# Batch 0's gate in one VectorE multiply in a Fourier-mixing and gated-convolution kernel

## The chip, the cores and the metric

The kernel runs on one core of one Trainium2 chip. The core has a matrix engine (TensorE, PE in the profile; its weight loads are listed apart as PEld), VectorE (DVE), ScalarE (ACT), GpSimd (POOL) and SyncE (SP), which only issues transfers. Each engine works through its own list of instructions in the order in which the program wrote them and waits on semaphores where an operand isn't ready. GpSimd also issues the transfers that accumulate into memory and those that gather by index. The metric is the device time of one execution in microseconds (us).

## The reference

Two blocks follow each other on 8 batches of 3136 x 256 float32 values. The first keeps the real part of a two-dimensional Fourier transform. The second projects to 1024 features, takes the positive part `h`, convolves it along the sequence with three taps per feature, squashes the sum with a sigmoid, multiplies that with `h` and projects back.

```python
X = np.fft.fft(np.fft.fft(x, axis=1), axis=2).real
h = np.maximum(X @ w_in, 0.0)
conv_out = sum(conv_w[k] * hp[:, k:k + S, :] for k in range(3))   # hp: h with a zero row at both ends
gate = 1.0 / (1.0 + np.exp(-conv_out))
return h * gate @ w_out
```

## The kernel before

**Transform.** The transform along the sequence is made from folded halves of `x` (VectorE adds and subtracts mirrored rows: lines 157, 160, 168, 172, 173; lines 194 and 195 make the sums and differences over features; line 228 turns two of the pieces) and from small matrix products with cosine and sine tables. Its result for one batch, the tiles `pt` and `qt`, is ready before that batch's second block starts. The transform along the features is folded into the first projection's weights, the tile `G`.

**Second block.** It is cut into steps `(b, c, f)`: batch, one of 4 chunks of the sequence, one of 8 groups of 128 features; 32 steps per batch and 256 in all. A step's tile is 128 features by 770 positions, or 832 in the last chunk of a batch. These are its parts, with their lines:

- `products` (TensorE, two matmuls into `pa` and two into `pb`), after `seed` (ScalarE, line 816) has put a first term into `pa`;
- `copies` (ScalarE, line 837, two per step) move `pb` to `nb`; `combine` (VectorE, line 845, two per step) reads `pa` from the matmul's memory and `nb`, and writes `h`, the positive part of their sums in the order of the sequence;
- the three taps: `first_tap` (ScalarE, line 851) writes `g`, `middle` (line 855) is a transfer that GpSimd issues and that adds a shifted `h` to `g` in memory, `last_tap` (VectorE, line 860) adds the last;
- `sigmoid` (ScalarE, line 875, two operations per step) and `gate`: GpSimd (line 883) multiplies one half of `g` by `h` and VectorE (line 884) the other;
- `mm2` (TensorE, 12 matmuls `po<-wout,g`) projects back; after the eighth group of features ScalarE copies `po` out (line 908).

**Order.** The order of the work is written out by hand. One loop runs over cycles `t`, and in a cycle each part belongs to another step, so that every engine finds work whose inputs came a cycle earlier:

```python
sigmoid(steps[t - 4]); products(steps[t + 1]); copies(steps[t + 1])
combine(steps[t]); seed(steps[t + 2]); first_tap(steps[t])
run("dve"); last_tap(steps[t - 3]); gate(steps[t - 4])
row_of(steps[t + 1]); middle(steps[t]); run("pool"); run("load"); mm2(steps[t - 5]); run("pe")
```

So VectorE's list in a cycle is `combine`, then side work, then `last_tap`, then `gate`. GpSimd's is `gate`, in some cycles a small `memset` (line 822), the issue of `middle`, then its own side work, among it the gathers of `x` for a later batch (line 132). Side work is hung on cycles by the table `side`. In batch 0's steps (cycles 0 to 35) it is: turning the output weights `wout` into float32 (VectorE lines 654, 662, 668, 669, 677), the folds and the products of batch 1's transform, and the first folds of batch 2's. The tiles `h` have 6 buffers and the tiles `g` 7.

Of the kernel before, what the change touches and what calls it, by code (L numbers as in the profile page):

```python
# [13 lines left out]
ALU = mybir.AluOpType  # L14
# [23 lines left out]
def kernel(  # L38
# [48 lines left out]
    vt = nc.vector.tensor_tensor  # L87
# [7 lines left out]
    def spare():  # L95

        return pso.tile([P, 2, D], F32, name="po", tag="po").rearrange("p a d -> p (a d)")
# [764 lines left out]
    def shares(s):  # L862


        ch = chunks[s[1]]
        w = ch.w - 2
        n = ch.rest[0] if ch.last else w
        m = n - n // 2
        return slice(0, m), slice(m, n), slice(n, w)

    def sigmoid(s):

        v, p, r = shares(s)
        for c in (slice(p.start, r.stop), v):
            act(gs[s][:, c], gs[s][:, c], AF.Sigmoid, scale=cw[:, 1, s[2]:s[2] + 1])  # L875

    def gate(s):

        b, c, f = s
        g, h = gs[s], hs.pop(s)[:, 1:]  # L880
        v, p, r = shares(s)
        p = slice(p.start, r.stop)
        gt(g[:, p], g[:, p], h[:, p], op=ALU.mult)  # L883
        vt(g[:, v], g[:, v], h[:, v], op=ALU.mult)  # L884
# [83 lines left out]
    for i, u in enumerate(us[j] for j in (4, 2, 3, 7, 8)):  # L968
        u.matmuls(0, 1)
        if i == 0:  # L970
            p = spare()
# [111 lines left out]
    for t in range(n + LAG):  # L1083
# [3 lines left out]
        if 0 <= t - 4 < n:  # L1087
            sigmoid(steps[t - 4])
# [17 lines left out]
        if 0 <= t - 4 < n:  # L1106
            gate(steps[t - 4])
# [75 lines left out]
```

## Time and profile before

| | |
|---|---|
| median of 3 runs | 1167.69 us (1164.38 to 1167.98) |
| the profiled execution | 1167.47 us, span of its instructions 1165.7 us |
| granted TensorE clock | 0.997 |
| TensorE busy | 1143.1 us, 98% of the span |
| VectorE busy | 978.5 us, 84% |
| ScalarE busy | 943.7 us, 81% |
| GpSimd busy | 604.7 us, 52% |
| batch 0's gates on GpSimd | 32, from 62.3 us to 203.5 us |
| batch 0's gates on VectorE | 32, from 63.2 us to 206.1 us |

An engine's busy time counts an instruction from its start to its end, and with it the time for which the instruction had started and could not go on. An idle time before an instruction is put down to the instruction that ended last of those it waited for. In rows that list instructions in order of time the columns are start (us from the span's start), duration (us), engine, line, operation, tiles and shape, how many were merged, and in brackets the idle time before with what ended it.

### The profile page before, as it was taken

To read this page: it belongs to the slowest core of one execution; us is meant where nothing else is said; L and a number is where in the kernel's file an instruction comes from. 1 tells how busy PE (TensorE), PEld (TensorE's weight loads), DVE (VectorE), ACT (ScalarE), POOL (GpSimd) and SP (SyncE) were. 2 spreads that over 40 slices of the span, in tenths; PEclk is the share of its full clock that TensorE was granted. 3 is DMA by queue.
4 is the path that set the end of the run, shared out by engine and by line. 5 is a ranking of instruction groups with operands and counts; after the bars stand their busy time and mean duration, and the time that the engine had idled before them with its cause. 6 is when DMAs were issued, how large, how long until landed. Compare 5 with 4: busy or idle time off the path is not lost.

```text
span 1165.7 us, 15936 instructions
## 1 busy us (share of the span) xinstructions
PE 1143.1 (98%) x4834; PEld 892.4 (77%) x4834; DVE 978.5 (84%) x1449; ACT 943.7 (81%) x1950; POOL 604.7 (52%) x741
## 2 busy tenths in 40 slices
PE   6989999999999999999999999999999999999998
PEld 4767787778777777778777777777777787777777
DVE  8799989997887889898877879779787777888885
ACT  3589877888888879887878888888887888898885
POOL 7356545665466464646365464745344444454443
PEclk9899999999999999999999999999999999999999
DMA  9767886777667686757675766865565556666654
GB/s 247 152 111 172 163 149 145 165 164 162 135 142 164 128 192 127 177 112 168 144 173 126 153 132 133 178 130 122 130 130 99 120 122 143 136 127 130 127 115 102
DMA packets 107602, 167.54 MB, mean 144 GB/s; under 512 B 32104, under 2 KB 62838, under 8 KB 107517
## 3 DMA queue, kind: packets, MB, share of 16 engines
q0 software_dynamic: 42160, 115.87, 52.0%
q1 hardware_dynamic: 64616, 50.53, 15.7%
q8 instruction: 38, 0.62, 0.2%
q14 instruction: 47, 0.39, 0.1%
q10 hardware_dynamic: 741, 0.14, 0.1%
HBM read 37.80 MB, written 25.74 MB: 55 GB/s over the span
## 4 chain that ended last, share of the span: by engine, by line
PE 79%; ACT 5%; DVE 4%; issue 2%; DVEq 0%; ACTq 0%
PE po L93 50%; PE pb L93 12%; PE pa L93 12%; PE pd L93 6%; DVE g L860 1%; ACT g L875 1%; ACT nb L837 1%; ACT os L908 1%; ACT pa L816 0%; DVE h L845 0%; ACT g L851 0%; DVE g L884 0%; DVE xh L168 0%; DVE w L194 0%; DVE xh L157 0%
## 5 line engine op out<-in xcount | busy, mean ns | idle before, releaser
L93 PE MATMUL po<-wout,g 128*128 128x256 f32 x3072 | 706.5, 379 | 5.3 <-DVE g L884 4.5
L93 PEld LDWEIGHTS po<-wout,g 128*128 128x128 f32 x3072 | 580.5, 190 | 150.8 <-issue 19.4
L855 POOL DMA_DIRECT2D g<-h x256 | 227.4, 888 | 470.0 <-ACT g L851 293.5
L875 ACT ACTIVATE g<-g,cw 128x385 f32<-128x385 f32 (+2 forms) x512 | 292.3, 625 | 67.2 <-DVE g L860 66.3
L883 POOL TENSOR_TENSOR g<-g,h 128x385 f32<-128x385 f32 (+1 forms) x256 | 294.5, 1151 | 44.5 <-ACT g L875 42.8
L837 ACT ACTIVATE nb<-pb 128x386 f32<-128x386 f32 (+3 forms) x512 | 227.0, 498 | 109.5 <-PE pb L93 108.9
L845 DVE CUSTOM_DVE_ANT_0 h<-pa,nb 128x386 f32<-128x386 f32 (+3 forms) x512 | 264.4, 556 | 28.1 <-POOL h L822 19.0
L860 DVE SCALAR_TENSOR_TENSOR g<-h,cw,g 128x770 f32<-128x770 f32 (+1 forms) x256 | 282.4, 1103 | 0.0
L851 ACT ACTIVATE g<-h,cw 128x770 f32<-128x770 f32 (+1 forms) x256 | 244.4, 955 | 0.0
L93 PE MATMUL pb<-qt,G 127*128 127x387 f32 (+2 forms) x512 | 214.5, 500 | 2.8 <-ACT nb L837 2.4
L93 PE MATMUL pa<-pt,G 128*128 128x387 f32 (+2 forms) x512 | 212.3, 495 | 0.5 <-ACT pa L816 0.5
L884 DVE TENSOR_TENSOR g<-g,h 128x385 f32<-128x385 f32 (+1 forms) x256 | 189.9, 742 | 24.6 <-ACT g L875 24.4
L816 ACT ACTIVATE pa<-eb,ge 128x387 f32<-128x387 f32 (+2 forms) x256 | 155.4, 607 | 1.5 <-DVE h L845 1.2
L93 PEld LDWEIGHTS pa<-pt,G 128*128 128x128 f32 x512 | 97.1, 190 | 74.7 <-issue 18.4
L132 POOL DMA_INDIRECT xh<-in_x_dram,idx x64 | 91.0, 1421 | 20.1 <-issue 11.4
L93 PEld LDWEIGHTS pb<-qt,G 127*128 127x128 f32 x512 | 91.1, 190 | 10.5 <-ACT nb L837 5.0
L93 PE MATMUL pd<-tab,w 98*128 98x197 f32 (+2 forms) x448 | 97.7, 317 | 0.2 <-DVE as L428 0.2
L93 PEld LDWEIGHTS pd<-tab,w 98*128 98x128 f32 (+1 forms) x448 | 81.9, 191 | 9.5 <-ACT pa L816 0.6
L908 ACT COPY os<-po 128x256 f32<-128x256 f32 x196 | 57.3, 393 | 6.5 <-PE po L93 6.5
L157 DVE TENSOR_TENSOR xh<-xh 98x1020 f32<-98x1020 f32 (+1 forms) x32 | 48.2, 1509 | 0.8 <-DMA xh<-in_x_dram,idx 0.7
L168 DVE TENSOR_TENSOR xh<-xh 98x1024 f32<-98x1024 f32 (+1 forms) x32 | 48.5, 1517 | 0.1
L194 DVE TENSOR_TENSOR w<-xh 98x508 f32<-98x508 f32 (+1 forms) x32 | 35.1, 1097 | 0.1
(149 smaller groups left out, 438.8 us busy)
## 6 DMA issues: line engine op xcount, KB each, us to landing
g<-h POOLq DMA_DIRECT2D x192, 385.0 KB, 4.0
g<-h POOLq DMA_DIRECT2D x64, 416.0 KB, 4.1
out_dram<-os SPq DMA_DIRECT2D x96, 256.0 KB
xh<-in_x_dram SPq DMA_DIRECT2D x16, 784.0 KB
eb<-ed SPq DMA_DIRECT2D x16, 193.5 KB
raw<-in_moe_w_in_dram SPq DMA_DIRECT2D x4, 512.0 KB
raw<-in_moe_w_out_dram SPq DMA_DIRECT2D x1, 2048.0 KB
eb<-ed SPq DMA_DIRECT2D x8, 209.0 KB
```

Of the source, the lines that this page charges most:

```text
L93: nc.tensor.matmul(o, l, r, start=start, stop=stop, skip_group_check=True)
L132: nc.gpsimd.indirect_dma_start(out=xh[b, h][0:NP, 7 - m].rearrange("p q d -> p (q d)"), out_offset=None, in_=bass.AP(tensor=x.tensor, offs ...
L816: act(pa[s][:, 0:n], eb[b, c], AF.Copy, scale=ge[:, f:f + 1])
L837: act(nb[s][:, i, cols], p[:, cols], AF.Copy, scale=-1.0 if i else 1.0)
L845: nc.vector._custom_dve(TENSOR_ADD_SAT, out=to, in0=a[:, cols], in1=c[:, i, cols], s0=BIG, s1=0.0)
L851: act(gs[s], hs[s][:, 0:n], AF.Copy, scale=cw[:, 0, s[2]:s[2] + 1])
L855: nc.gpsimd.dma_start(out=gs[s], in_=hs[s][:, 1:1 + n], accum_op=ALU.add)
L860: stt(out=g, in0=h[:, k:k + n], scalar=cw[:, k, f:f + 1], in1=g, op0=ALU.mult, op1=ALU.add)
L875: act(gs[s][:, c], gs[s][:, c], AF.Sigmoid, scale=cw[:, 1, s[2]:s[2] + 1])
L883: gt(g[:, p], g[:, p], h[:, p], op=ALU.mult)
L884: vt(g[:, v], g[:, v], h[:, v], op=ALU.mult)
L908: nc.scalar.copy(out=osb[:, j % 2], in_=pt[:, j % 2])
```

## The change

For steps of batch 0 (`s[0] == 0`) the gate is one VectorE multiply over the whole tile, 770 or 832 columns, and GpSimd gets no multiply; the sigmoid of such a step is one ScalarE operation over the whole tile in place of two over its halves. Steps of batches 1 to 7 are as before.

```diff
+    def whole(s):
+
+        return s[0] == 0
+
     def sigmoid(s):
 
         v, p, r = shares(s)
-        for c in (slice(p.start, r.stop), v):
+        for c in [slice(0, r.stop)] if whole(s) else (slice(p.start, r.stop), v):
             act(gs[s][:, c], gs[s][:, c], AF.Sigmoid, scale=cw[:, 1, s[2]:s[2] + 1])
 
     def gate(s):
...
         v, p, r = shares(s)
+        if whole(s):
+            vt(g, g, h[:, 0:r.stop], op=ALU.mult)
+            return
         p = slice(p.start, r.stop)
         gt(g[:, p], g[:, p], h[:, p], op=ALU.mult)
         vt(g[:, v], g[:, v], h[:, v], op=ALU.mult)
```

Here is GpSimd's list around the gathers (L132) of the first half of batch 2's rows of `x`, some 120 to 135 us into the span; before the change it reads:

```order
L883 TENSOR_TENSOR g<-g,h 128x385
L855 DMA g<-h 128x770
L883 TENSOR_TENSOR g<-g,h 128x385
L855 DMA g<-h 128x770
L132 DMA xh<-in_x_dram,idx 98x512
L883 TENSOR_TENSOR g<-g,h 128x385
L855 DMA g<-h 128x770
```

and after it:

```order
L855 DMA g<-h 128x770 x2
L132 DMA xh<-in_x_dram,idx 98x512
L855 DMA g<-h 128x770
L132 DMA xh<-in_x_dram,idx 98x512
L855 DMA g<-h 128x770
```

The multiply is gone from every cycle; the gathers and the issues of `middle` follow each other in the same order as before.

VectorE's list at about the same place, two cycles of it (L157, L160 and L168 are folds, side work of batch 1's transform; the program's list calls the last tap a TENSOR_SCALAR and `combine` an ISA), reads before:

```order
L157 TENSOR_TENSOR xh<-xh 99x4x255
L160 TENSOR_TENSOR xh<-xh 99x8
L860 TENSOR_SCALAR g<-h,cw,g 128x770
L884 TENSOR_TENSOR g<-g,h 128x385
L845 ISA h<-pa,nb 128x386 x2
L168 TENSOR_TENSOR xh<-xh 99x1024
```

and after the change:

```order
L157 TENSOR_TENSOR xh<-xh 99x4x255
L160 TENSOR_TENSOR xh<-xh 99x8
L860 TENSOR_SCALAR g<-h,cw,g 128x770
L887 TENSOR_TENSOR g<-g,h 128x770
L845 ISA h<-pa,nb 128x386 x2
L168 TENSOR_TENSOR xh<-xh 99x1024
```

Each gate stands where it stood, with 770 columns in place of 385; nothing else moves on VectorE.

## The prediction

> **What bounds the kernel now.** I read the page's busy times first, and then busy time by stretch, cut at the starts of four `mm2` groups:
>
> ```profile
> PE 1143.1 (98%) x4834; PEld 892.4 (77%) x4834; DVE 978.5 (84%) x1449; ACT 943.7 (81%) x1950; POOL 604.7 (52%) x741
> ```
>
> ```profile
> 63.15:138.75 75.60, 71.79 (x290) 52.83 (x290) 74.77 (x108) 65.16 (x144) 44.99 (x58) 1.00 0.71 149
> 138.75:207.20 68.45, 68.45 (x304) 53.98 (x305) 61.79 (x99) 53.41 (x112) 34.41 (x45) 1.00 0.78 143
> 207.20:241.03 33.83, 32.49 (x130) 23.89 (x129) 33.03 (x44) 27.52 (x57) 21.83 (x28) 1.00 0.74 165
> ```
>
> The columns are the stretch, its length, and the busy time of PE, PEld, DVE, ACT, POOL. Over the whole run TensorE is the bound (98%). The first two stretches hold all of batch 0's gates. In the first, VectorE is busy for 74.77 of 75.60 us and TensorE stands idle for 3.8 us. In the second TensorE is never idle and VectorE has 6.7 us to spare. In the third, already batch 1, VectorE is full again and TensorE is idle for 1.3 us. Who ends TensorE's waits in the first and in the third stretch:
>
> ```profile
> PE po L93 <- DVE g L884: 2.6, 4, 1.5
> ```
>
> ```profile
> PE po L93 <- DVE g L884: 1.3, 4, 0.6
> ```
>
> It is VectorE's gate, 2.6 us in the first and 1.3 us in the third. Here are one `mm2` group each of two undisturbed cycles, then the first and the last group of the first stretch:
>
> ```profile
> 126.64 2.75 PE L93 MATMUL po<-wout,g 128*128 128x256 f32 x12
> ...
> 130.54 2.75 PE L93 MATMUL po<-wout,g 128*128 128x256 f32 x12
> ```
>
> ```profile
> 64.97 2.75 PE L93 MATMUL po<-wout,g 128*128 128x256 f32 x12
> ```
>
> ```profile
> 138.75 0.48 PE L93 MATMUL po<-wout,g 128*128 128x256 f32 x1 [0.22 <-DVE g L884]
> ```
>
> TensorE needs 3.90 us per cycle when nothing stops it; the 17 cycles from 64.97 to 138.75 took 73.8 us and not 66.3 (small products of the border features take part of the rest). So in the first stretch VectorE sets the pace, and the question is what VectorE's full 75 us consist of. The next rows are from VectorE's and GpSimd's lists in order of time:
>
> ```profile
> 130.63 2.28 DVE L168 TENSOR_TENSOR xh<-xh 99x1024 f32<-99x1024 f32 x1
> 132.84 1.01 DVE L860 SCALAR_TENSOR_TENSOR g<-h,cw,g 128x770 f32<-128x770 f32 x1
> 133.77 0.55 DVE L884 TENSOR_TENSOR g<-g,h 128x385 f32<-128x385 f32 x1
> ```
>
> ```profile
> 129.86 1.05 POOL L132 DMA_INDIRECT xh<-in_x_dram,idx  x1 [0.30 <-issue]
> 130.93 0.90 POOL L883 TENSOR_TENSOR g<-g,h 128x385 f32<-128x385 f32 x1
> ```
>
> ```profile
> 95.82 1.21 DVE L168 TENSOR_TENSOR xh<-xh 98x1024 f32<-98x1024 f32 x1
> ```
>
> The same fold of 1024 columns took 1.21 us at 95.82, with GpSimd not multiplying, and 2.28 us at 130.63. GpSimd's multiply ended at 131.83, and the fold ended 1.08 us after that: it stood still until GpSimd had finished and then ran. So "busy" VectorE time holds standstill behind GpSimd's half of the gate. Other rows show that GpSimd's issue of `middle` (L855) does not do this:
>
> ```profile
> 72.45 0.88 POOL L855 DMA_DIRECT2D g<-h  x1 [1.09 <-ACT g L851]
> ...
> 72.51 1.02 DVE L860 SCALAR_TENSOR_TENSOR g<-h,cw,g 128x770 f32<-128x770 f32 x1
> ```
>
> The last tap under it took 1.02 us, as long as without it (1.01 at 132.84).
>
> [...]
>
> **The change part by part.** *What VectorE gains.* These are the groups of the first stretch (63.1 to 139.5 us) in which an operation was held up: busy time, then the mean ns of one.
>
> ```profile
> L884 DVE TENSOR_TENSOR g<-g,h 128x385 f32<-128x385 f32 x18 | 10.6, 588 | 0.3 <-ACT g L875 0.3
> L157 DVE TENSOR_TENSOR xh<-xh 99x1020 f32<-99x1020 f32 x2 | 3.6, 1800 | 0.0
> L228 DVE SCALAR_TENSOR_TENSOR w<-w,turn,rt 98x256 f32<-98x256 f32 x2 | 3.4, 1722 | 0.0
> L168 DVE TENSOR_TENSOR xh<-xh 98x1024 f32<-98x1024 f32 x2 | 3.3, 1638 | 0.0
> L662 DVE SCALAR_TENSOR_TENSOR wout<-raw,wout 128x512 int32<-128x512 int32 x3 | 3.1, 1048 | 0.0
> L668 DVE TENSOR_SCALAR left<-raw 128x512 int32<-128x512 int32 x3 | 3.0, 996 | 0.0
> L168 DVE TENSOR_TENSOR xh<-xh 99x1024 f32<-99x1024 f32 x1 | 2.3, 2283 | 0.0
> L195 DVE TENSOR_TENSOR w<-xh 98x508 f32<-98x508 f32 x2 | 2.0, 1010 | 0.0
> L654 DVE TENSOR_SCALAR wout<-raw 128x512 int32<-128x512 int32 x3 | 1.9, 640 | 0.0
> L194 DVE TENSOR_TENSOR w<-xh 99x508 f32<-99x508 f32 x1 | 1.5, 1521 | 0.0
> ```
>
> And these are the same operations undisturbed (two groups of 73 to 80 us, and two rows in order of time):
>
> ```profile
> L662 DVE SCALAR_TENSOR_TENSOR wout<-raw,wout 128x512 int32<-128x512 int32 x1 | 0.7, 679 | 0.0
> L668 DVE TENSOR_SCALAR left<-raw 128x512 int32<-128x512 int32 x1 | 0.4, 419 | 0.0
> ```
>
> ```profile
> 119.49 0.68 DVE L195 TENSOR_TENSOR w<-xh 98x508 f32<-98x508 f32 x1
> ```
>
> ```profile
> 145.72 0.99 DVE L228 SCALAR_TENSOR_TENSOR w<-w,turn,rt 98x256 f32<-98x256 f32 x2
> ```
>
> Standstill is count times (mean less undisturbed): L884 18 x 0.04 = 0.7; L157 2 x 0.59 = 1.2 (1.21 us taken from the fold of 1024); L228 3.4 - 1.0 = 2.4; L168 2 x 0.43 + 1.07 = 1.9; L662 3 x 0.37 = 1.1; L668 3 x 0.58 = 1.7; L195 2 x 0.33 = 0.7; L654 3 x 0.22 = 0.7 (0.42 as L668); L194 0.84. The sum is 11.2 us.
>
> *What of it stays.* The gathers (L132) hold VectorE too: the fold at 130.63 began 0.28 us before the gather ended. Four of the stretch's seven gathers were running when the held operation behind them began; at 0.28 us each 1.1 us stays. The bounds are 0 and, if all seven hold for a whole gather of 1.05 us, 7.4 us.
>
> *What VectorE pays.* A multiply took 0.55 us for 385 columns (133.77) and 1.21 us for 1024 (95.82), so a column costs 0.66 / 639 us and 385 more cost 0.40 us. The upper bound is the last tap's 1.01 us for 770 columns, 0.46 more. I take 0.40, the row of the same operation. 18 gates up to 138.75 cost 7.2 us (8.3 at most). The net on VectorE is 7.2 + 1.1 - 11.2 = -2.9 us, and as VectorE sets the pace there, the `mm2` of 138.75 comes 2.9 us sooner.
>
> *The second stretch* costs nothing on the path as long as its cover holds. 14 gates there add 8 x 0.46 (832 columns) + 6 x 0.40 = 6.1 us to VectorE; the cover is its 6.7 us of idle time, and standstill that goes here too (139.5 to 206 us):
>
> ```profile
> L168 DVE TENSOR_TENSOR xh<-xh 98x1024 f32<-98x1024 f32 x2 | 3.0, 1492 | 0.0
> L194 DVE TENSOR_TENSOR w<-xh 98x508 f32<-98x508 f32 x1 | 2.2, 2220 | 0.0
> L172 DVE TENSOR_TENSOR xh<-xh 98x512 f32<-98x512 f32 x1 | 2.0, 2008 | 0.0
> ```
>
> That is 2 x 0.28 + 1.54 + 1.33 = 3.4 us (0.68 us undisturbed for the last two). Without the cover, 6.1 us would come on the path. TensorE carries the 2.9 us through this stretch.
>
> *The third stretch.* The 3.4 us lie behind 178 us, where VectorE has no idle time left, against six gates by 0.46 = 2.8 us before the last one. VectorE so enters the third stretch some 0.6 us further ahead of TensorE, and up to 1.3 us of TensorE's waits can shrink. I take 0.8 us, between 0 and 1.3.
>
> *Sigmoid in one operation.* ScalarE's list shows two halves, and one operation of the full width:
>
> ```profile
> 79.57 0.93 ACT L851 ACTIVATE g<-h,cw 128x770 f32<-128x770 f32 x1
> 81.02 1.12 ACT L875 ACTIVATE g<-g,cw 128x385 f32<-128x385 f32 x2 [0.52 <-DVE g L860]
> ```
>
> That is 0.19 us less per step for an engine which is idle before it; I take nothing for it. The gate needs the whole sigmoid, but it stands last in VectorE's cycle, behind `combine` and side work.
>
> *GpSimd* loses 32 multiplies and gets nothing; its `middle` and gathers can only be ready sooner. A gather may wait for VectorE longer (last tap and gate now follow each other for 1.8 us), and behind it waits the next `middle`, needed three cycles later, so this is hidden by more than 8 us.
>
> **Sum.** -2.9 - 0.8 = -3.7 us. The profiled execution's own time is 1167.47 us, 0.22 below the median of 1167.69; against the median this gives 1164.0 us.
>
> **The rivals.**
>
> *VectorE only gets more work (slower).* The engine that sets the pace gets 7.2 us more in the first stretch. If the standstill stays, because GpSimd's gathers and issues take the multiply's place, the `mm2` of 138.75 comes 7.2 us later, and 1.5 us may follow at 207: 1175 to 1176 us. It decides from the point where more than 4.0 of the 11.2 us stays (11.2 - 7.2). For it speaks the gather's 1.05 us ahead of the fold at 130.63; against it the undisturbed last tap beside L855, and that a gather stands in only 7 of 18 cycles.
>
> [...]
>
> *The gain is taken up elsewhere (no change).* VectorE comes free sooner but waits for `nb` and `pa` (ScalarE is busy for 65 of 75.6 us), or the lead is lost again by 207. Then it is 1166.5 to 1168.5 us. Against it: VectorE's idle time in the first stretch is 0.8 us, so ScalarE is rarely late now.
>
> *All of TensorE's idle time goes.* 3.8 + 1.3 = 5.1 us, and up to 7.5 if all that the 17 cycles took over 66.3 us goes: 1160.2 to 1162.6 us. It needs VectorE to stay ahead of TensorE in every cycle, and cycles with a fold of 1.21 us and two weight operations leave no room for it.
>
> **How the numbers follow.** About 0.3%, 3.5 us, is what a measurement of this kernel can tell from no change. My forecast has a chance of 0.55, with a range of its own of 1162.6 to 1166; two thirds of it (0.35) are beyond the 3.5 us, 0.20 within. All idle time gone has 0.08 (faster), the gain taken up 0.14 (within), more work only 0.23 (slower). So faster 0.43, same 0.34, slower 0.23. The range goes down to 1160.0, the third rival's end, and up to 1171.0: every gather holding VectorE for its whole 1.05 us adds 7.4 - 1.1 = 6.3 us to the forecast, and half of the first rival's 7.2 us on the median ends there too.
>
> **What would show it.** In the profile after: VectorE's gate at about 0.95 us for 770 columns; L168 and L157 near 1.2 us and L668 near 0.42 in all their rows; L228's pair near 1 us; TensorE's idle time before the `mm2` groups up to 139 us shrunk, and the group now at 138.75 near 135.8; the distance from there to the end as before. It would be wrong if VectorE's side work keeps its long rows with L132 or L855 in front, or if the gate over 770 columns is itself held up.

## The result

| | before | after |
|---|---|---|
| median of 12 runs | 1165.07 us | 1161.84 us |
| lowest | 1164.38 us | 1161.41 us |
| the profiled execution | 1167.47 us | 1164.74 us |

The ratio after to before is 0.9974, with a 95% interval of 0.9964 to 0.9985: 3.2 us faster, against 3.7 forecast. The time itself, 1161.84 us, is 2.2 us below the forecast's 1164.0, because the three runs that the forecast started from had a median of 1167.69 and these twelve have one of 1165.07. Nearly all runs lie on one of two levels some 3 us apart, with a mean granted clock of 0.999 to 1.0 on the lower and of 0.993 to 0.997 on the upper, so a difference in microseconds below is that between the medians of the lower levels, against the kernel before measured beside it (1161.80 and 1164.92, so -3.1 us for the change), while a ratio takes all runs.

Busy time by stretch in the profile after, cut at 63.15 us, which in both profiles lies ahead of the first `mm2` group (64.97), and at the same three groups as before (columns: stretch, length, busy PE, PEld, DVE, ACT, POOL):

```profile
63.15:136.82 73.67, 71.45 (x290) 52.93 (x291) 72.91 (x111) 62.98 (x129) 34.05 (x38) 1.00 0.71 151
136.82:205.75 68.93, 68.88 (x306) 53.70 (x305) 61.17 (x98) 50.87 (x97) 23.41 (x32) 1.00 0.79 144
205.75:238.19 32.44, 31.41 (x130) 24.14 (x128) 31.42 (x42) 27.32 (x57) 26.15 (x27) 1.00 0.78 172
```

The lengths were 75.60, 68.45 and 33.83. So the first stretch gave 1.93 us, the second cost 0.48, the third gave 1.39: 2.84 us by 238 us; the profiled executions differ by 2.73. Behind it nothing changed (924.57 us before, 924.71 after).

These are VectorE's groups of the first stretch, after (63.1 to 137.5 us; mean ns behind the busy time):

```profile
L887 DVE TENSOR_TENSOR g<-g,h 128x770 f32<-128x770 f32 x19 | 18.2, 955 | 0.6 <-ACT g L879 0.6
...
L168 DVE TENSOR_TENSOR xh<-xh 99x1024 f32<-99x1024 f32 x2 | 2.4, 1217 | 0.0
L168 DVE TENSOR_TENSOR xh<-xh 98x1024 f32<-98x1024 f32 x2 | 2.4, 1216 | 0.0
...
L157 DVE TENSOR_TENSOR xh<-xh 99x1020 f32<-99x1020 f32 x2 | 2.4, 1212 | 0.0
...
L662 DVE SCALAR_TENSOR_TENSOR wout<-raw,wout 128x512 int32<-128x512 int32 x3 | 2.0, 683 | 0.0
...
L194 DVE TENSOR_TENSOR w<-xh 98x508 f32<-98x508 f32 x2 | 1.4, 678 | 0.0
L668 DVE TENSOR_SCALAR left<-raw 128x512 int32<-128x512 int32 x3 | 1.3, 442 | 0.0
...
L228 DVE SCALAR_TENSOR_TENSOR w<-w,turn,rt 98x256 f32<-98x256 f32 x2 | 0.9, 477 | 0.0
```

Every group that was held up is at its undisturbed time: 1217 ns where it was 2283, 442 where it was 996, 477 where it was 1722. The gate takes 955 ns, 0.40 us more than its half did. Now VectorE at the end of the stretch: the gate of step 17, and the next wait; after,

```profile
133.33 0.96 DVE L887 TENSOR_TENSOR g<-g,h 128x770 f32<-128x770 f32 x1
...
142.82 0.36 DVE L401 TENSOR_TENSOR as<-as,pd 128x196 f32<-128x196 f32 x1 [3.72 <-ACT as L397]
```

and before:

```profile
138.15 0.55 DVE L884 TENSOR_TENSOR g<-g,h 128x385 f32<-128x385 f32 x1
...
145.18 0.36 DVE L401 TENSOR_TENSOR as<-as,pd 128x196 f32<-128x196 f32 x1 [0.80 <-issue]
```

The gate ends at 134.29 and not at 138.70, 4.4 us sooner, yet the `mm2` group that reads it starts only 1.93 us sooner (136.82). VectorE then waits 3.72 us where it waited 0.80. It has gained more than was forecast, and TensorE has taken less than half of it. TensorE's waits in the first stretch after (63 to 139 us) are:

```profile
PE po L93 <- DVE g L887: 1.1, 1, 1.1
PE pb L93 <- ACT nb L837: 0.7, 1, 0.7
PE pa L93 <- ACT pa L816: 0.7, 2, 0.4
```

The wait for `pb` lies ahead of the first group (63.56 us). One wait for the gate is left, before the group at 86.13, in the cycle with two weight operations and a fold. Then TensorE waits for ScalarE's `pa`, and from 108 us on it runs at its own pace, 3.90 us per cycle and what the border features add.

One wait is new in this stretch. GpSimd's small copy into the folded halves (L179, 4 columns), ScalarE behind it and TensorE behind that:

```profile
103.68 2.14 POOL L179 COPY w<-xh 98x4 f32<-98x4 f32 x1
```

```profile
105.89 0.91 ACT L222 ACTIVATE rt<-w,turn 98x256 f32<-98x256 f32 x2 [1.53 <-POOL w L181]
106.70 0.56 ACT L816 ACTIVATE pa<-eb,ge 128x387 f32<-128x387 f32 x1
```

```profile
107.32 0.92 PE L93 MATMUL pa<-pt,G 128*128 128x387 f32 x2 [0.29 <-ACT pa L816]
```

In the kernel before, the same copy took 1.38 us, ScalarE waited 0.60 us for it, and TensorE did not wait. Here it ended at 105.82, while `combine` ran (from 105.68): VectorE's fold, last tap and gate stood back to back from 102.74 on, and now it is GpSimd that is shut out.

### The profile page after: what moved, and what is told of

It is laid out like the page before. It is cut to its first block, busy times and chain, and to the rows that moved or that the text cites. A ratio compares the mean times of both kernels' runs of the same rounds, so it can differ in the third digit from the quotient of the medians.

```text
span 1163.0 us, 15837 instructions
## 1 busy us (share of the span) xinstructions
PE 1142.7 (98%) x4834; PEld 893.1 (77%) x4834; DVE 973.3 (84%) x1449; ACT 939.3 (81%) x1918; POOL 586.9 (50%) x709
## 4 chain that ended last, share of the span: by engine, by line
PE 86%; DVE 5%; ACT 4%; issue 2%; POOL 1%; DMA 1%; ACTq 0%; POOLq 0%; DVEq 0%
PE po L93 54%; PE pb L93 13%; PE pa L93 13%; PE pd L93 6%; DVE g L860 1%; ACT nb L837 1%; ACT os L915 1%; DMA xh<-in_x_dram 1%; POOL xh L132 1%; ACT g L879 1%; DVE h L845 1%; DVE g L887 1%; ACT pa L816 0%; DMA tab<-dft_seq_dram 0%; DVE g L891 0%
## 5 line engine op out<-in xcount | busy, mean ns | idle before, releaser
L879 ACT ACTIVATE g<-g,cw 128x385 f32<-128x385 f32 (+3 forms) x480 | 286.3, 647 | 54.5 <-DVE g L860 53.4
L890 POOL TENSOR_TENSOR g<-g,h 128x385 f32<-128x385 f32 (+1 forms) x224 | 261.5, 1168 | 36.4 <-ACT g L879 35.1
L891 DVE TENSOR_TENSOR g<-g,h 128x385 f32<-128x385 f32 (+1 forms) x224 | 172.3, 769 | 24.3 <-ACT g L879 24.1
L132 POOL DMA_INDIRECT xh<-in_x_dram,idx x64 | 98.3, 1536 | 19.8 <-issue 11.5
L157 DVE TENSOR_TENSOR xh<-xh 98x1020 f32<-98x1020 f32 (+1 forms) x32 | 44.0, 1377 | 0.6 <-DMA xh<-in_x_dram,idx 0.4
L168 DVE TENSOR_TENSOR xh<-xh 98x1024 f32<-98x1024 f32 (+1 forms) x32 | 43.6, 1361 | 0.1
L401 DVE TENSOR_TENSOR as<-as,pd 128x196 f32<-128x196 f32 x14 | 5.0, 358 | 38.4 <-ACT as L397 38.4
```

The lines of the kernel that those rows point to most:

```text
L132: nc.gpsimd.indirect_dma_start(out=xh[b, h][0:NP, 7 - m].rearrange("p q d -> p (q d)"), out_offset=None, in_=bass.AP(tensor=x.tensor, offs ...
```

## The experiments

The theory was: GpSimd's multiply holds up VectorE's operations (the fold of 1024 columns took 2.28 us behind it and 1.21 without it); taking the multiply away frees VectorE of standstill that is worth more than the multiply. The rivals were that ScalarE's merged sigmoid makes the gain, or GpSimd's emptier queue. Differences are to the kernel before unless said otherwise.

### Which half of the change it is

Gate alone (the sigmoid stays in halves):

```diff
-        for c in [slice(0, r.stop)] if whole(s) else (slice(p.start, r.stop), v):
+        for c in (slice(p.start, r.stop), v):
```

> Half of the change: in batch 0 VectorE multiplies the whole gate and GpSimd none, but the sigmoid stays two operations per step. Theory (VectorE's standstill behind GpSimd's multiply goes): nearly the whole gain, 2 to 3.5 us faster than before, and VectorE's folds at 1.2 us. Rival (the gain is ScalarE's, 0.19 us per step from the merged sigmoid): within 1 us of before.

Measured: -2.9 us (ratio 0.9983, 0.9971 to 0.9994; by the ratio 2.0 us). Sigmoid alone (the gate split as before):

```diff
-        if whole(s):
-            vt(g, g, h[:, 0:r.stop], op=ALU.mult)
-            return
```

> The other half: in batch 0 the sigmoid is one operation per step, and the gate is split between GpSimd and VectorE as before. Theory (standstill): within 1 us of before, with VectorE's folds held up to 2.3 us again. Rival (ScalarE's saving makes the gain): 2 to 3 us faster than before.

Measured: -0.1 us (0.9999, 0.9988 to 1.0010). The folds of 1024 columns in the two profiles (min, median and max ns), with the gate alone and then with the sigmoid alone:

```profile
L168 DVE TENSOR_TENSOR xh<-xh x6: 1214/1218/1225, 95.2 to 192.4; 98x1024 f32<-98x1024 f32 x4, 99x1024 f32<-99x1024 f32 x2
```

```profile
L168 DVE TENSOR_TENSOR xh<-xh x6: 1208/1954/2482, 93.5 to 191.1; 98x1024 f32<-98x1024 f32 x4, 99x1024 f32<-99x1024 f32 x2
```

The gain comes with the gate's half of the change, and the standstill is gone with that half alone. ScalarE's part is 0.1 to 0.2 us, too little for these runs to tell from nothing.

### Is it that GpSimd reads, or that it is busy?

A multiply on GpSimd that nobody needs is put back in the first 18 steps:

```diff
         if whole(s):
+            if steps.index(s) < 18:
+                dummy = left[:, 0:NF // 2].rearrange("p f i -> p (f i)")[:, 0:p.stop - p.start]
+                gt(dummy, h[:, p], h[:, p], op=ALU.mult)
             vt(g, g, h[:, 0:r.stop], op=ALU.mult)
             return
```

> The changed kernel, and in the first 18 steps GpSimd multiplies again where it did before, 385 columns of h by themselves into a tile that is free there; nobody needs the result. VectorE pays for the whole gate and GpSimd reads the memory as before. Theory (two readers exclude each other): the standstill of some 10 us comes back on top of VectorE's 7.2 us, so 5 to 9 us slower than before, 8 to 12 us slower than the changed kernel. Rival (the gain came from GpSimd's halves no longer being waited for, or from the merged sigmoid): within 1.5 us of the changed kernel.

Measured: +9.0 us (1.0088, 1.0068 to 1.0108; by the ratio 10.3 us), some 12 us above the changed kernel, at the upper end of what was expected or beyond it. Its six runs spread over 6 us, and the profile is of the slowest. The stretches of this profile:

```profile
65.95:147.80 81.85, 72.43 (x286) 52.69 (x287) 79.46 (x106) 61.50 (x125) 50.52 (x52) 0.98 0.62 133
147.80:220.95 73.15, 70.86 (x306) 54.84 (x305) 63.74 (x101) 51.27 (x97) 27.62 (x35) 0.98 0.73 134
```

From the first `mm2` group to that of step 17 it is 81.85 us; in the changed kernel it was 71.85 (64.97 to 136.82). Two of VectorE's operations, and the dummy multiplies themselves, in this profile (63.1 to 148 us):

```profile
L157 DVE TENSOR_TENSOR xh<-xh 98x1020 f32<-98x1020 f32 x2 | 3.8, 1892 | 0.0
...
L172 DVE TENSOR_TENSOR xh<-xh 98x512 f32<-98x512 f32 x1 | 2.1, 2097 | 0.0
```

```profile
L889 POOL TENSOR_TENSOR left<-h 128x385 f32<-128x385 f32 x17 | 25.2, 1480 | 0.1
```

VectorE stands still again (1892 ns for 1212; 2097 for 0.68 us), though at other operations, because this multiply does not wait for the sigmoid and runs at another time. GpSimd stands still too (1480 ns in the mean and 821 to 3702 ns for one and the same multiply, where that of the kernel before took 1045 in the mean), and what queues behind it is late: a copy kept ScalarE, and TensorE behind it, waiting at the start of the second stretch, which is 4.2 us longer than in the changed kernel:

```profile
153.46 0.91 ACT L222 ACTIVATE rt<-w,turn 98x256 f32<-98x256 f32 x2 [4.92 <-POOL w L181]
```

Some 3 us of the profile are TensorE's clock: it was 0.83 from 90 to 100 us and from 150 to 160 us (an estimate: 0.17 of twice 10 us), 0.98 over each of the two stretches. Another 0.7 us of the first stretch is `combine` waiting until the dummy multiply has read a buffer of `h`. So with the multiply back both engines have standstill, VectorE 1892 ns for 1212 and GpSimd 1480 for 1045; as a price of VectorE's standstill alone the 9.0 us is too high.

The same place on the queue, with a write in the multiply's stead:

```diff
-                gt(dummy, h[:, p], h[:, p], op=ALU.mult)
+                for _ in range(2):
+                    nc.gpsimd.memset(dummy, 0.0)
```

> The changed kernel, and in the first 18 steps GpSimd fills the same free tile twice with zeros (385 columns each) where it multiplied before: about as long on GpSimd's queue, but it reads nothing. Theory (only a GpSimd operation that reads the memory excludes VectorE's operations with two inputs there): within 1 us of the changed kernel. Rival (anything that GpSimd executes holds VectorE up, or GpSimd's queue sets the pace): 3 us or more slower than the changed kernel.

Measured: -2.7 us (0.9984, 0.9971 to 0.9997), 0.4 above the changed kernel. GpSimd's fills, and VectorE's folds beside them:

```profile
L890 POOL MEMSET left<- 128x385 f32 x36 | 18.6, 518 | 1.0
```

```profile
L168 DVE TENSOR_TENSOR xh<-xh x6: 1210/1214/1219, 95.7 to 192.8; 98x1024 f32<-98x1024 f32 x4, 99x1024 f32<-99x1024 f32 x2
```

GpSimd was as busy as with its multiply in the kernel before (18.6 us, where that took 18.8) and VectorE's folds show no standstill: those of 1024 columns took 1210 to 1219 ns, and L157's of 1020 columns 1208 to 1217, where two took 1892 in the mean beside the dummy multiply. For these folds, which have two inputs in memory, it is the multiply, which reads, that holds them, not a busy queue. That only operations with two inputs are held is not shown: L654 and L668, which the multiply had held up too, have one (640 and 996 ns before, 419 and 442 after the change). Beside the fills L654 still took 514 ns, one of its three rows 0.70 us, so for these the run does not show that reading is all.

### How much of VectorE's room TensorE can take

Here the other half of the product is left out in batch 0, so VectorE's gate is as short as before and GpSimd has none:

```diff
         if whole(s):
-            vt(g, g, h[:, 0:r.stop], op=ALU.mult)
+            vt(g[:, v], g[:, v], h[:, v], op=ALU.mult)
             return
```

> The changed kernel with VectorE multiplying only its old half in batch 0; the other half of the gate's product is left out, so VectorE pays nothing for what GpSimd no longer does. It asks how much of a faster VectorE TensorE can take. Theory that VectorE still sets the pace after the change: 0.40 us times 18 gates = 7.2 us more room, so 2.5 us or more faster than the changed kernel. Rival (TensorE and ScalarE now set the pace, VectorE's new room is idle time): 0.5 to 1.5 us faster than the changed kernel, from the one wait of 1.1 us on the gate that is left at 86 us.

Measured: -6.6 us (0.9941, 0.9926 to 0.9956), 3.5 us faster than the changed kernel.

```profile
64.75:133.80 69.05, 68.90 (x287) 52.63 (x286) 64.82 (x108) 61.08 (x126) 28.50 (x38) 1.00 0.74 158
133.80:202.15 68.35, 68.35 (x306) 53.87 (x304) 55.36 (x99) 50.59 (x97) 21.09 (x32) 1.00 0.78 144
202.15:234.50 32.35, 31.41 (x129) 24.14 (x128) 31.69 (x41) 27.31 (x57) 24.92 (x27) 1.00 0.79 172
```

TensorE is idle for 0.15 us of the first stretch. From `mm2` to `mm2` it takes 69.05 us, against 71.85 in the changed kernel and 73.78 before: so VectorE still set the pace in part of the stretch after the change. Two thirds of the way (2.0 of 2.8 us) are made up to the ninth group, at 98 us in the changed kernel, where its cycle is longer than 3.90 us. The first theory held, and 3.5 us is what the gate's other half still costs, its hold on GpSimd included (the small copies took 0.5 to 1.4 us in this run).

### Which steps

`whole(s)` true for the first 18 steps only, and for the last 14 of batch 0 only:

```diff
-        return s[0] == 0
+        return steps.index(s) < 18
```

> The change for batch 0's first 18 steps alone, those of the first stretch; the other 14 are split as before. Theory: the first stretch's gain as in the changed kernel, some 1.9 us at the mm2 group of step 17, and nothing or little behind it: 1.5 to 2.5 us faster than before in all. Rival (the gain is made in the third stretch, by the lead that the second gives): under 1 us faster than before.

```diff
-        return s[0] == 0
+        return 18 <= steps.index(s) < 32
```

> The change for batch 0's last 14 steps alone. Theory: no gain up to the mm2 group of step 17, then VectorE's lead into batch 1: 0.5 to 1.5 us faster than before. With the other part it should add up to the whole change, about 3.3 us. Rival (the second stretch is hidden on both sides): 0 us.

Measured: -2.2 us (0.9981, 0.9972 to 0.9991) and -0.6 us (0.9998, 0.9989 to 1.0007, by itself not clear of the noise), -2.8 together, where the whole change gave -3.1. With the first 18 the stretches took 71.89, 68.35 and 33.86 us, with the last 14 73.94, 69.04 and 32.45. So the second stretch's 0.5 us is a price of its own gates, and the third stretch's 1.4 us is their gain: the two add up within what the runs tell.

### The copies that GpSimd makes late

Batch 1's four small copies on VectorE:

```diff
-                    nc.gpsimd.tensor_copy(w[k, 0:2, qs, 0], t()[k, s:s + 2, :, 0])
+                    (nc.vector if b == 1 else nc.gpsimd).tensor_copy(w[k, 0:2, qs, 0], t()[k, s:s + 2, :, 0])
```

> The changed kernel, with the four small copies of batch 1's transform (4 columns each) made by VectorE and not by GpSimd. In the changed kernel such a copy took 2.14 us at 103.7 us behind VectorE, and ScalarE waited 1.5 us for it, then TensorE for pa. Theory (the new wait of the change is GpSimd's copies shut out by VectorE): ScalarE's waits for them go and it is 0.5 to 1.7 us faster than the changed kernel. Rival (those waits are covered): within 0.3 us of the changed kernel, or slower by VectorE's extra 0.4 to 0.6 us.

Measured: -3.8 us (0.9970, 0.9961 to 0.9979), 0.7 us faster than the changed kernel. ScalarE's row no longer has a wait:

```profile
101.28 0.93 ACT L222 ACTIVATE rt<-w,turn 98x256 f32<-98x256 f32 x2
```

The first stretch shrank from 71.85 to 71.26 us. The new wait was real and cost about 0.6 us. With all later batches' copies on VectorE (`if b else` in the same line):

> The changed kernel, with the four small copies of every later batch's transform made by VectorE, not only batch 1's. Theory (such a copy matters only where VectorE is full, so in batch 0's steps): as the kernel with batch 1's copies alone, 0.4 to 1 us faster than the changed kernel. Rival (ScalarE waits for them everywhere): 1.5 us or more faster than the changed kernel.

Measured: -4.0 us (0.9964, 0.9951 to 0.9978): no more than 0.2 us beyond batch 1's. The changed kernel does wait for another of these copies, batch 2's third, in the third stretch:

```profile
228.21 0.91 ACT L222 ACTIVATE rt<-w,turn 98x256 f32<-98x256 f32 x2 [2.58 <-POOL w L181]
```

```profile
229.65 0.92 PE L93 MATMUL pa<-pt,G 128*128 128x387 f32 x2 [1.03 <-ACT pa L816]
```

With all copies on VectorE this wait is gone from the profile, but TensorE waits 0.61 us for a gate at 234.49 us instead, and the stretch takes 31.92 us where it took 32.44.

### More batches

`return s[0] < 2`, and `return True`:

> The change for batches 0 and 1. In the profile of the changed kernel TensorE is idle for only 1.0 us in the first 32 us of batch 1. Theory (what the change gives is bounded by TensorE's waits for VectorE, and batch 1 has few left): within 0.8 us of the changed kernel. Rival (each batch gives what batch 0 gave): 2 to 3 us faster than the changed kernel.

> The change for all eight batches; GpSimd multiplies nowhere. VectorE pays 0.40 us more in each of 224 further steps, some 90 us, and its gates there lose 0.22 us of standstill each, some 49 us, beside what its other operations lose. Theory (TensorE sets the pace from batch 1 on, so VectorE's extra work is hidden and there is little to win): within 2 us of the changed kernel. Rival (VectorE becomes the bound where its standstill was short): 5 us or more slower than the changed kernel.

Measured: -3.7 us (0.9957, 0.9941 to 0.9973) and -3.2 us (0.9969, 0.9955 to 0.9982). Batch 1 adds 0.6 us, and with its gates on VectorE the third stretch takes 31.15 us in the profile, without a wait of TensorE; the other six batches take 0.5 back. Both are within what these runs resolve. TensorE sets the pace there, and some 90 us more of multiplying on VectorE (an estimate, 224 gates by 0.40 us) do not show: its busy time in the profile even fell, from 973.3 to 957.5 us, as the standstill of its other operations went. All batches with all copies on VectorE:

> The change for all eight batches, and all later batches' small copies on VectorE: GpSimd then reads the memory only for its gathers. Theory (the copies are the one place where GpSimd is still shut out and waited for): 0.4 to 1 us faster than the change for all batches without them. Rival (covered behind batch 0): the same as without them within 0.3 us.

Measured: -4.2 us (0.9946, 0.9928 to 0.9964), 1.0 us better than without the copies. It has the lowest median of all complete kernels here, 1160.77 us, and GpSimd's busy time is 352.4 us where it was 604.7. Against the kernels with batch 1's gates, batch 1's copies or all copies added alone, its lead of 0.2 to 0.5 us is within what these runs resolve.

## Why the prediction was right, and where its steps were off

**Right:** the sign, the mechanism and the size to 0.6 us, though the size partly by luck, as its three terms were off by more and to different sides. The likelier part of the forecast, a gain beyond 3.5 us, did not come. What VectorE was forecast to pay (0.40 us per gate) is what it pays, 955 ns against 0.55 us. What it was to gain, 11.2 us of standstill over ten groups, went in every one of them. The dummy multiply (1892 ns for the fold of 1020 columns) and the fills (1208 to 1217 ns for it) show that GpSimd's multiply was the cause and not a GpSimd that is busy.

**Off: the gathers' 1.1 us "stays".** Nothing stayed. In the profile after, a gather and a fold start together and neither is held:

```profile
94.86 1.08 POOL L132 DMA_INDIRECT xh<-in_x_dram,idx  x1 [0.30 <-issue]
```

```profile
94.94 1.22 DVE L168 TENSOR_TENSOR xh<-xh 98x1024 f32<-98x1024 f32 x1
```

The prediction charged the gather for the 0.28 us by which the fold at 130.63 began before the gather's end; the fold did stand still for longer there (1.07 us) than the multiply is recorded (0.90), but with the multiply gone no group is held, so all of it went. What stopped the fold beyond the multiply's record is not shown. Without this term the sum gives -4.0 us for VectorE; measured at the gate of step 17 it was -4.4.

**Off: "as VectorE sets the pace there, the `mm2` of 138.75 comes 2.9 us sooner".** It came 1.9 us sooner. VectorE set the pace only up to about 98 us. Behind that the freed time became idle time of VectorE (3.72 us where it had been 0.80), because TensorE waited for `pa`, first behind ScalarE's own work and then behind GpSimd's late copy, and then had its own 3.90 us per cycle. The step took a stretch of 75 us as one regime by its mean. This error and the one before point to opposite sides, and so do the two below: the three stretches came to -1.9, +0.5 and -1.4 us where the forecast had -2.9, 0 and -0.8, together -2.8 for -3.7.

**Off: the second stretch "costs nothing".** It cost 0.5 us. Its idle time lies where VectorE waits for ScalarE, not in every cycle, and in a full cycle the longer gate is what `mm2` waits for. Gate, and `mm2` group:

```profile
182.18 1.02 DVE L887 TENSOR_TENSOR g<-g,h 128x832 f32<-128x832 f32 x1
```

```profile
183.26 2.86 PE L93 MATMUL po<-wout,g 128*128 128x256 f32 x12
```

The group starts 0.06 us after the gate's end, 4.11 us after the one before it; the same two groups were 3.89 us apart before. The group at 153.05 us starts 0.05 us after its gate's end as well. These two cycles and the one behind each took 0.57 us more than before.

**Off: the third stretch's 0.8 us** was 1.4, just beyond the upper bound of 1.3. The bound was TensorE's recorded idle time, and that shows less than a wait costs: against eight cycles of 3.90 us the stretch lost 2.6 us before, with 1.3 us of idle time on record, because the records of undisturbed matmuls overlap by some 0.16 us, those on both sides of a wait do not, and the group behind it is recorded as longer (2.86 us for 2.75). All four waits for the gate went, and the one for `pa` behind GpSimd's copy (1.03 us) took the place of some of them.

**The rivals.** More work alone, slower: this is what the dummy multiply brings about, +9.0 us where the rival said 7 to 9, with other waits in it. The gain taken up elsewhere: it happened to more than half of VectorE's gain. All of TensorE's idle time gone: no, because of the one cycle at 86 us and the waits for `pa`; with half the product left out it does go, at -6.6 us. That GpSimd has nothing to lose was wrong: what it still reads comes later (batch 1's copies took 1.4 to 2.6 us and not 0.5 to 1.4), and the forecast that this was hidden looked at the gathers and `middle` alone and missed the copies.

## What to carry to other kernels

Busy time of VectorE can hold standstill (1.21 and 2.28 us for one fold here): compare the shortest with the mean duration of one shape before calling the engine full. Half an operation given to GpSimd here took 0.40 us off VectorE and cost it 0.6 us (11.2 us over 18 multiplies) elsewhere, so count the operations that it holds up, not only the one that it takes over. When such a share is taken back, look for small operations that GpSimd still makes and that somebody waits for, and value freed time cycle by cycle by what the next engine can take.

## What the runs showed that was not expected

**A halved clock.** In some of the profiled executions TensorE's granted clock is halved early in the span: it is 0.50 in each window from 40 to 45 us in the kernel before and from 37 to 46 us in the changed kernel, and 1.00 from 30 to 50 us with the merged sigmoid alone. By the clock from 30 to 40 and from 40 to 50 us (0.93 and 0.73 before, 0.84 and 0.65 after) the halving lasts some 7 and 10 us, an estimate. The same 24 matmuls, in the profiled execution of the kernel before, and in that of the one with the merged sigmoid alone, where the clock stayed whole:

```profile
37.28 6.14 PE L93 MATMUL po<-tab,w 98*128 98x197 f32 x24
```

```profile
36.83 3.96 PE L93 MATMUL po<-tab,w 98*128 98x197 f32 x24
```

The first `mm2` group then starts at 64.97 us and not at 61.99, 3 us later. What starts the halving is not shown. In the dummy multiply's profile the clock also fell to 0.52 (92 to 94 us) right behind a wait of TensorE of 3.57 us for a gate, and the `mm2` group there took 4.29 us where the others of its stretch took 2.75 to 2.86; from 20 to 37 us, in the profile of the kernel before, the longest wait is 0.55 us.

**Who is shut out.** It is not always the same engine. With GpSimd's multiply in its list VectorE lost 11.2 us in 75; without it, with last tap and gate back to back, GpSimd's gathers rose from 1404 to 1879 ns in the mean (63 to 139 us) and its small copies, 0.5 to 1.4 us before, to 1.9 to 2.6 us, while VectorE lost nothing that shows (its folds of 1024 columns took 1203 to 1218 ns).
